# Adding two of VectorE's three exponent readings by a DMA that GpSimd starts, in a fused attention and feed-forward kernel

## The chip, the cores and the metric

The kernel runs on one core of a Trainium2 chip. The metric is device time in microseconds (us) of one execution; the time before is the median of three runs. Five engines each run their own in-order list: TensorE (PE in the profile, with PEld for its weight loads), VectorE (DVE), ScalarE (ACT), GpSimd (POOL) and SyncE (SP, which here only starts DMAs). They wait for each other by semaphores.

## The reference

```python
xn = (x - mean) / sqrt(var + 1e-5)                # x: 2048 tokens x 640, bfloat16
q = xn @ wq ; k = xn @ wk ; v = xn @ wv           # 32 query heads of 20, one key and one value head
p = softmax(q k^T / sqrt(20))                     # for each head, 2048 x 2048
attn = concat(p @ v) @ wo
ffn = silu(xn @ w1) @ w2                          # hidden size 1728
out = x + attn + ffn
```

## The kernel before

A scheduler in Python lays out every instruction ahead of time. It keeps a list of pending operations with an assumed duration, a priority and the operations that they depend on, plays the five engines forward, and writes each engine's list in the order that comes out. A table of 64 rows (`SEG`), one for each 32 score blocks, gives thresholds that steer it (when a block goes to VectorE, when the values' matmuls may interrupt, and so on). On the chip the lists are fixed, and only semaphore waits move them.

The work. A prologue loads x in 16 tiles of 128 tokens, computes their mean and variance (on VectorE, or on ScalarE for the tiles in `ACT_STATS`), takes the root by a Newton iteration of some ten small GpSimd instructions (`newton`), normalises, transposes (by TensorE or by a DMA transpose, the tiles in `DT`), and projects keys, values and the first queries.

The main part walks over 2048 score blocks, each 128 keys x 512 queries of one head. A step of TensorE (`do_S`, line 1133) computes 3 or 4 of them, side by side in four row strips of its array, into PSUM banks. The exponential is taken in one of two ways:

- ScalarE reads 1 to 3 banks at once and writes exp as bfloat16 into the tile E (line 1167, `sbt10`).
- VectorE, for about a third of the blocks, reads one bank and writes it clamped as int16 into Z (line 1182, `sbt11`). The bits of that integer, read as a bfloat16, are an approximate exponential. To smooth its error the kernel uses three readings of it: Z itself, and Z with two constants added (the tile Y, `sbt12`). Z has four sets of three blocks each; when a set is full, `flush_z` orders the two additions for the whole set, one on GpSimd (line 1221, two blocks of additions in 64-bit words) and the other on GpSimd or VectorE (line 1215).

The values' matmuls (`do_pv`, line 973; "PV" below) multiply E, Z and Y blocks by the values and sum in PSUM, up to four matmuls side by side in four column strips of the array, one for each head of a group. A block of ScalarE needs one matmul. A block of VectorE needs three, one for each reading, each with its own copy of V, scaled by the reading's weight (`PH`): these are entries of one list, `self.item(...)`, from which `do_pv` takes what is ready.

In the gaps the scheduler sets the query projections, the feed-forward layers and the output projection (line 872), tanh for the SiLU on ScalarE (line 1379) and its product on VectorE (line 1384). After the last score block a short tail ends the output.

Of a DMA the scheduler assumes, in `commit`, that what it brings is there 2.0 us plus the operation's own `late` after its issue has ended. Other engines' lists are built on that.

Of the kernel before, what the change touches and what calls it, by code (L numbers as in the profile page):

```python
# [8 lines left out]
BF16 = mybir.dt.bfloat16  # L9
# [39 lines left out]
OFF_LO = 45.0  # L49
PH = ((0, 1.0), (43, 0.8046875), (86, 0.625))  # L50
# [11 lines left out]
H0_STEP = 10  # L62
# [25 lines left out]
FOUR_FROM = 35  # L88
# [7 lines left out]
PV_HOLD = 12  # L96
# [3 lines left out]
DT = (5, 6, 7, 8, 9, 10, 11, 12, 14, 15)  # L100
NORM_P = 0.9
# [13 lines left out]
STD_COST = 7.4  # L115
K1_ENG = "pool"
PV_MIN = 3
PV_GO = 9
PRO = "t0 t2 t1 p0 t3 k0 k1 p1 q1 v0 t4 k2 v1 k3 k4 t13 v2 k5 k6 v3 k7 d0"
ACT_STATS = (1, 4, 6, 12, 14, 15)  # L120
NW_ENG = ("pool", "pool", "pool")
NORM_ENG = ("pool", "dve", "dve", "dve", "pool", "dve", "dve", "dve", "dve", "pool", "dve", "pool")
# [5 lines left out]
            "ACT4", "SPLIT", "U2", "LOOK", "JOB_BANKS", "U_IDLE")  # L128
SEG = (
# [64 lines left out]
)  # L194
BATCHES = ((0, 4), (4, 10), (10, 16))
T_ACT = (0, 2, 6)


class Op:
# [1741 lines left out]
```

## Time and profile before

| | |
|---|---|
| median of 3 runs | 662.31 us (662.22 to 662.44) |
| profiled execution, time | 662.48 us |
| profiled execution, span | 660.7 us |
| granted TensorE clock | 1.000 |
| TensorE busy | 654.3 us |
| ScalarE busy | 645.8 us |
| VectorE busy | 601.5 us |
| GpSimd busy | 420.3 us |

The span runs from the first to the last instruction; the time of the same execution is 1.8 us longer. "Busy" is the union of an engine's instructions; consecutive instructions on ScalarE and TensorE overlap at their ends, so the mean duration of one is longer than the distance from one start to the next. In rows of groups the columns are: busy us, mean ns of one, idle time of the engine just ahead, and what ended most of that idle time.

### The profile page before, as it was taken

The numbers are of one execution on the slowest core, as the hardware profiler recorded it, in microseconds if no ns is written. First come the engines' busy times: TensorE is split into PE (matmuls) and PEld (weight loads), VectorE is DVE, ScalarE is ACT, GpSimd is POOL, SyncE is SP. The second block draws the span as 40 slices with busy tenths as digits, with TensorE's granted clock in tenths as the row PEclk, the third lists the DMA queues.
The fourth block names the chain that finished last, engine by engine and source line by source line (L and its number), as shares of the span: only waits on it lengthen the run. The fifth ranks groups of instructions, "written<-read, shape, count | busy, mean of one in ns | idle before, by whom it ended". The sixth has DMA issues, their size and how long they took to land.

```text
span 660.7 us, 22924 instructions
## 1 busy us (share of the span) xinstructions
PE 654.3 (99%) x9762; PEld 220.6 (33%) x9764; DVE 601.5 (91%) x1060; ACT 645.8 (98%) x735; POOL 420.3 (64%) x568
## 2 busy tenths in 40 slices
PE   8999999999999999999999999999999999999998
PEld 4432222323333333333333333333332333333334
DVE  7799999899999997999999979999999998999995
ACT  7899999999999999999999999999999999999995
POOL 6646667676776662676666744677666664766673
PEclk9999999999999999999999999999999999999999
DMA  7566300000004200001003210000000310011001
GB/s 212 97 237 195 88 18 11 10 13 13 14 20 72 73 10 10 10 10 18 18 11 57 63 39 10 18 10 8 12 19 10 77 55 25 10 18 34 11 10 42
DMA packets 52058, 27.89 MB, mean 42 GB/s; under 512 B 37910, under 2 KB 51318, under 8 KB 51958
## 3 DMA queue, kind: packets, MB, share of 16 engines
q1 hardware_dynamic: 50502, 26.22, 15.6%
q8 instruction: 78, 1.28, 0.8%
q10 hardware_dynamic: 1456, 0.22, 0.2%
q14 instruction: 22, 0.18, 0.1%
HBM read 11.44 MB, written 2.62 MB: 21 GB/s over the span
## 4 chain that ended last, share of the span: by engine, by line
PE 92%; ACT 3%; DVE 2%; DMA 2%; SPq 1%; issue 0%; DVEq 0%
PE psall L973 34%; PE psall L1133 29%; PE psall L872 27%; ACT sbt L1167 3%; DMA sbt<-sbt 1%; DVE sbt L1685 1%; DMA sbt<-in_A_x_dram 1%; SPq L1575 0%; DVE sbt L1715 0%; PE psall L1828 0%; PE psall L1369 0%; PE psall L1851 0%; ACT sbt L1379 0%; DVE sbt L1467 0%; DVE sbt L1820 0%
## 5 line engine op out<-in xcount | busy, mean ns | idle before, releaser
L1167 ACT ACTIVATE sbt<-psall 128x1024 bf16<-128x1024 f32 (+2 forms) x644 | 609.6, 1068 | 3.5 <-PE psall L1133 2.9
L1221 POOL INT64_ADD sbt<-sbt x491 | 394.1, 815 | 209.1 <-DVE sbt L1182 183.8
L1182 DVE TENSOR_SCALAR sbt<-psall 128x512 int16<-128x512 f32 x739 | 476.4, 684 | 37.1 <-PE psall L1133 27.6
L973 PE MATMUL psall<-sbt 128*32 128x512 bf16 x3526 | 266.7, 383 | 0.0
L1133 PE MATMUL psall<-sbt 32*128 32x512 bf16 x2048 | 243.6, 384 | 0.3 <-ACT sbt L1167 0.2
L872 PE MATMUL psall<-sbt 128*32 128x320 bf16 (+2 forms) x3939 | 218.3, 331 | 0.3 <-DVE sbt L1687 0.3
L1133 PEld LDWEIGHTS psall<-sbt 32*128 32x128 bf16 x2048 | 61.8, 91 | 235.2 <-issue 80.8
L872 PEld LDWEIGHTS psall<-sbt 128*32 128x32 bf16 x3939 | 85.6, 95 | 85.1 <-issue 50.2
L973 PEld LDWEIGHTS psall<-sbt 128*32 128x32 bf16 x3526 | 63.3, 95 | 99.5 <-issue 68.9
L1384 DVE SCALAR_TENSOR_TENSOR sbt<-sbt,psall 128x512 bf16<-128x512 bf16 x54 | 36.7, 682 | 6.5 <-ACT sbt L1379 6.0
L1379 ACT ACTIVATE sbt<-psall 128x512 bf16<-128x512 f32 x54 | 33.6, 629 | 0.4 <-PE psall L872 0.3
L1285 DVE CAST sbt<-psall 128x512 bf16<-128x512 f32 x32 | 21.9, 683 | 0.6 <-PE psall L973 0.4
L1275 DVE TENSOR_TENSOR sbt<-sbt 128x320 bf16<-128x320 bf16 x31 | 15.8, 510 | 0.0
L1448 DVE SCALAR_TENSOR_TENSOR sbt<-psall,sbt 128x320 bf16<-128x320 f32 x28 | 13.5, 484 | 1.6 <-PE psall L872 1.2
L848 PE MATMUL psall<-sbt 128*128 128x512 bf16 (+2 forms) x44 | 12.9, 447 | 1.4 <-DVE sbt L1624 1.2
L1467 DVE SCALAR_TENSOR_TENSOR sbt<-psall,sbt 128x320 bf16<-128x320 f32 x28 | 13.0, 482 | 1.2 <-PE psall L872 1.2
L1336 DVE TENSOR_SCALAR sbt<-psall 128x512 bf16<-128x512 f32 (+1 forms) x19 | 12.9, 678 | 0.1
L1685 DVE BATCH_NORM_STATS2 sbt<-sbt 128x6 f32<-128x320 bf16 x20 | 8.9, 471 | 3.4 <-DMA sbt<-in_A_x_dram 3.4
L1269 DVE RECIPROCAL sbt<-sbt 128x16 f32<-128x16 bf16 x31 | 7.6, 244 | 0.4 <-DMA sbt<-sbt 0.4
L848 PEld LDWEIGHTS psall<-sbt 128*128 128x128 bf16 x46 | 4.8, 112 | 7.5 <-issue 3.3
L1227 POOL TENSOR_TENSOR sbt<-sbt 128x768 int32<-128x768 int32 x4 | 5.9, 1465 | 0.5 <-DVE sbt L1182 0.5
L1464 ACT ACTIVATE sbt<-psall 128x320 bf16<-128x320 f32 x4 | 1.6, 437 | 4.4 <-PE psall L872 4.3
(72 smaller groups left out, 90.8 us busy)
## 6 DMA issues: line engine op xcount, KB each, us to landing
sbt<-in_A_x_dram SPq DMA_DIRECT2D x32, 160.0 KB, 3.7
out_dram<-sbt SPq DMA_DIRECT2D x15, 160.0 KB, 2.0
sbt<-in_B_w_dram SPq DMA_DIRECT2D x5, 432.0 KB, 5.3
sbt<-sbt SPq DMA_DIRECT2D x105, 20.0 KB
sbt<-in_B_w_dram SPq DMA_DIRECT2D x13, 160.0 KB, 3.0
sbt<-sbt SPq DMA_DIRECT2D x1, 1024.0 KB, 6.3
sbt<-sbt SPq DMA_TRANSPOSE x57, 2.5
sbt<-in_A_wo_dram SPq DMA_DIRECT2D x5, 160.0 KB, 3.0
```

The costliest lines, as they stand in the source:

```text
L848: return pe.matmul(self.bk(b, 0, n), self.zero[:, 0:P], self.zero[:, 0:n], start=True, stop=True)
L872: ins = pe.matmul(self.bk(b, 0, n, r, r + SLOT), w[:, r:r + SLOT], x, start=start, stop=stop, tile_position=(0, r), skip_group_check=True)
L973: ins = pe.matmul(self.bk(ub[k], 0, QW, r, r + SLOT), self.v[:, it.w, it.kt, :], it.x(), start=f, stop=False, tile_position=(0, r), skip_g ...
L1133: ins = pe.matmul(self.bk(bank[x]), self.kT[r:r + SLOT, kk, kt * P:(kt + 1) * P], self.qT[r:r + SLOT, g % 8, (g // 8) % 2, :], start=True, ...
L1167: return a.activation(self.E[:, b0 * QW:(b0 + na) * QW].rearrange("p (b n) -> p b n", n=QW), src, AF.Exp, scale=ACT_SCALE)
L1182: return v.tensor_scalar(self.Z[:, zs, zp * QW:(zp + 1) * QW], self.bk(bb), 0.0, ZMAX, ALU.max, ALU.min)
L1221: sc.new("pool", tp, lambda v, k=k, c=c: v.int64_add(self.Y[:, zs, k, 0:w].bitcast(I64), self.Z[:, zs, 0:w].bitcast(I64), c), zk + [("lib" ...
L1275: op = sc.new(eng, 0.067 + 16 * DH / 960.0, lambda v: v.tensor_tensor(dst, ut[:, :, :, 0:DH], rb, ALU.mult), [key, ("rL", up)], [("o", h0 ...
L1285: sc.new("dve", t_dve_ps(QW), lambda v: v.tensor_copy(self.U[:, up, :], self.bk(ub)), [("B", ub)], [("U", up)], prio=U_PRIO, name=f"Uev{g}")
L1379: sc.new("act", t_act(QW), lambda a: a.activation(t, src, AF.Tanh, scale=0.5), [("B", b)], [("tb", tp)], prio=TH_PRIO, name=f"th{c}_{fk}") ...
L1384: sc.new("dve", t_dve_ps(QW), lambda v: v.scalar_tensor_tensor(out=self.hT[0:rows, fk, :], in0=t, scalar=1.0, in1=src, op0=ALU.add, op1=AL ...
L1685: np_("dve", 0.41, lambda v, hf=hf: v.bn_stats(self.st6[:, n, hf, :], x[:, hf * 320:hf * 320 + 320]), self.xkeys(n), [("st6", n, hf)], pri ...
```

## The change

When a set of three VectorE blocks is full and both additions have been ordered, `flush_z` may now order one more operation on GpSimd: a DMA that adds Z to the first of the two Y readings, in bfloat16, in place (line 1239 of the changed kernel). For such a set the PV list gets two entries for a block, not three: the sum with one weight, and the second reading. For a set without the DMA it gets three, as before; Z and the first reading have the same weight, so that there are two copies of V. A new threshold `CB_TH` in the table decides for each set by how far GpSimd lags behind TensorE. 135 sets get the DMA.

The constants of the readings are new (`PH`, `PW`, `OFF_LO`), all 64 rows of the table are new (one is shown), and some thresholds. In the prologue GpSimd takes the root by one power instruction (`root`), the batches of tiles, the tiles of ScalarE's statistics (five for six) and the order of jobs (`PRO`) are others, and ScalarE's table load stands ahead of its two weight loads.

```diff
-OFF_LO = 45.0
-PH = ((0, 1.0), (43, 0.8046875), (86, 0.625))
+OFF_LO = 17.625
+PH = (0, 41, 87)
+PW = (1.0, 0.77734375)
...
-H0_STEP = 10
+H0_STEP = 20
...
-FOUR_FROM = 35
+FOUR_FROM = 15
...
-PV_HOLD = 12
+PV_HOLD = 16
...
-DT = (5, 6, 7, 8, 9, 10, 11, 12, 14, 15)
-NORM_P = 0.9
+DT = (4, 5, 7, 9, 10, 11, 12, 14, 15)
+NORM_P = 2.5
...
+POW_COST = 0.6
+CB_COST = 1.0
+CB_LATE = 1.0
+CB_PRIO = 3.0
+CB_TH = -9.0
...
-PRO = "t0 t2 t1 p0 t3 k0 k1 p1 q1 v0 t4 k2 v1 k3 k4 t13 v2 k5 k6 v3 k7 d0"
-ACT_STATS = (1, 4, 6, 12, 14, 15)
...
+PRO = "t2 t0 t1 p0 t3 k0 k1 p1 q1 t6 v0 k2 k3 t8 v1 t13 k4 k5 v2 k6 k7 v3 d0"
+ACT_STATS = (2, 4, 5, 12, 14)
...
-    (8.178, 1.808, 1.279, 0.2, 2, 4, 1, 2.527, 0.05, 0.93, 0.18, 32, 0.3, 0.573, 10, 6, 2, 54, 24, 30, 6, 0, 1, 0, 99, 0, 2, 0, -9),
+    (1.642, 0.699, 0.633, 0.313, 7, 5, 3, 2.06, 0.05, 0.14, 0.03, 23, 2.84, 1.295, 10, 6, 3, 54, 21, 33, 21, 0, 0, 0, 99, 0, 3, 16, 2.539),
...
-        self.v = sb([P, 3, KT, SLOT], BF16)
+        self.v = sb([P, 2, KT, SLOT], BF16)
...
-            self.item(g, j, kt, 0, lambda zs=zs, zp=zp: self.Z[:, zs, zp * QW:(zp + 1) * QW].bitcast(BF16),
-                      [("Z", zs, zp)])
...
+        both = n == ZB and self.wide and back["pool"] + 2 * tp - sc.t["pe"] < CB_TH
+        if both:
+            y0 = self.Y[:, zs, 0, 0:w].bitcast(BF16)
+            z0 = self.Z[:, zs, 0:w].bitcast(BF16)
+            yk = [("Y", zs, 0, i) for i in range(n)]
+            op = sc.new("pool", CB_COST, lambda q: q.dma_start(out=y0, in_=z0, accum_op=ALU.add), zk + yk, yk,
+                        prio=CB_PRIO, name="cb")
+            op.dma = op.lock = True
+            op.sem = self.s_cb[zs]
+            op.mode = 2 * P * w * 2
+            op.late = CB_LATE
...
         for i, (t, g, kt, j) in enumerate(self.zblocks):
+            if not both:
+                self.item(g, j, kt, 0, lambda i=i: self.Z[:, zs, i * QW:(i + 1) * QW].bitcast(BF16), [("Z", zs, i)])
             for k in range(2):
-                self.item(g, j, kt, k + 1, lambda k=k, i=i: self.Y[:, zs, k, i * QW:(i + 1) * QW].bitcast(BF16),
+                self.item(g, j, kt, k, lambda k=k, i=i: self.Y[:, zs, k, i * QW:(i + 1) * QW].bitcast(BF16),
                           [("Y", zs, k, i)])
...
+        def root(a, b_, pr):
...
+            add = np_("pool", 0.2, lambda g: g.tensor_scalar(ve, self.mv[:, a:b_, 1], EPS, None, ALU.add), mvk(a, b_),
+                      [("va", a)], prio=pr, name="eps")
+            add.then = np_("pool", POW_COST, lambda g: g.tensor_tensor(self.rstd[:, a:b_], ve, hb, ALU.pow),
+                           [("va", a), ("half",)], [("rs", a)], prio=pr, name="root")
```

What the new order does on the engines, as the two programs have it. The names: `sbt7` keys, `sbt8` the copies of V, `sbt9` queries, `sbt10` E, `sbt11` Z, `sbt12` Y; L1221 and L1225 are the same 64-bit addition (printed as ISA), two of them for a set of three blocks.

GpSimd's list in the second half of the main part, before:

```order
L1221 ISA sbt12<-sbt11 128x256 x2
L1221 ISA sbt12<-sbt11 128x768 x12
L1221 ISA sbt12<-sbt11 128x512 x2
L1221 ISA sbt12<-sbt11 128x768 x78
L1221 ISA sbt12<-sbt11 128x256 x2
L1221 ISA sbt12<-sbt11 128x768 x60
```

and in the change:

```order
L1225 ISA sbt12<-sbt11 128x768 x2
L1239 DMA sbt12<-sbt11 128x1536
L1225 ISA sbt12<-sbt11 128x768 x2
L1239 DMA sbt12<-sbt11 128x1536
L1225 ISA sbt12<-sbt11 128x768 x2
L1239 DMA sbt12<-sbt11 128x1536
L1225 ISA sbt12<-sbt11 128x768 x4
L1239 DMA sbt12<-sbt11 128x1536
```

Where long runs of additions stood, each pair of additions is followed by the start of a DMA of 128 x 1536 elements; in this stretch nearly every set has one.

TensorE's list in the same part of the program, before (L1133 are score steps, L973 PV matmuls):

```order
L1133 MATMUL psall<-sbt9,sbt7 128x512 x3
L973 MATMUL psall<-sbt10,sbt8 32x512
L973 MATMUL psall<-sbt11,sbt8 32x512
L973 MATMUL psall<-sbt10,sbt8 32x512
L973 MATMUL psall<-sbt12,sbt8 32x512
L973 MATMUL psall<-sbt11,sbt8 32x512
L973 MATMUL psall<-sbt10,sbt8 32x512
L973 MATMUL psall<-sbt12,sbt8 32x512 x2
L1133 MATMUL psall<-sbt9,sbt7 128x512 x3
```

and in the change (L1139 and L979):

```order
L1139 MATMUL psall<-sbt9,sbt7 128x512 x4
L979 MATMUL psall<-sbt10,sbt8 32x512 x2
L979 MATMUL psall<-sbt12,sbt8 32x512 x2
L979 MATMUL psall<-sbt10,sbt8 32x512
L979 MATMUL psall<-sbt12,sbt8 32x512 x3
L1139 MATMUL psall<-sbt9,sbt7 128x512 x3
```

The matmuls that read Z (`sbt11`) have gone from this place; those that read Y (`sbt12`) now depend on the DMA.

Instructions counted over both whole programs:

| | before | after |
|---|---|---|
| exp on ScalarE, 3 / 2 / 1 banks at once | 44 / 577 / 23 | 15 / 623 / 3 |
| blocks read by VectorE | 739 | 754 |
| first addition on VectorE | 5 | 9 |
| 64-bit additions on GpSimd | 491 | 494 |
| accumulating DMAs started by GpSimd | 0 | 135 |
| PV matmuls | 3526 | 3151 |
| PV steps (up to four matmuls side by side) | 889 | 818 |
| score steps (3 or 4 blocks) | 621 | 638 |
| tiles with statistics on ScalarE / VectorE | 6 / 10 | 5 / 11 |

More of the change, by code (lines that the diff above doesn't have):

```diff
@@ L115 @@
 STD_COST = 7.4
+POW_COST = 0.6
[3 more added lines that the diff above has]
+CB_TH = -9.0
+AG_NEXT = 3
 K1_ENG = "pool"
@@ L549, in alloc @@
         self.eps = sb([P, 1], F32)
+        self.half = sb([P, 1], F32)
         self.cy = sb([P, 2], I32)
@@ L1567, in prologue @@
         self.ut_cnt = [0, 0]
+        self.s_cb = [sem(f"cb{i}") for i in range(NZ)]
+        self.cb_cnt = [0] * NZ
         self.s_oT = [sem(f"oT{i}") for i in range(4)]
@@ L1576, in load_x @@
                         self.xkeys(n)[:2] if n < NT - 1 else self.xkeys(n)[:1], P * D * 2, sem=s_x[n])
-            op.late = 0.1 if n == 0 else 0.3 if n == 1 else 1.2 if n < 13 else 2.2
+            op.late = (0.1, 0.2, 0.4, 0.6)[n] if n < 4 else 1.4 if n < 13 else 2.2
             op.inc_no = 1
@@ L1587, in load_w @@
             sc.note(op, (), [tag])
+        sc.new("pool", 0.1, lambda g: g.memset(self.eps[:, :], EPS), [], [("eps",)], name="pool")
+        sc.new("act", 1.4, lambda ac: ac.activation(self.tmp[:, 1, 0:1], self.eps[:, :], AF.Exp), [("eps",)],
+               [("warm",)], prio=0.0, name="table")
         for src, k, j in ((self.A_wk, "k", 0), (self.A_wv, "v", 1)):
             sv = src.rearrange("(c p) d -> p c d", p=P)
-            load_w("act", k, [lambda q, sv=sv, j=j: q.dma_start(self.kv_st[:, j, :, :], sv)], ("st", k), 25600)
+            load_w("act", k, [lambda q, sv=sv, j=j: q.dma_start(self.kv_st[:, j, :, :], sv)], ("st", k), 25600, (),
+                   [("warm",)], 1.5 + j)
         for n in range(4):
@@ L1624, in prologue @@
         np_("dve", 0.3, lambda v: v.memset(self.zero[:, :], 0.0), [], [("zero",)], prio=-1.0, name="zero")
[L1625 removed]
+        pool(0.1, lambda g: g.memset(self.half[:, :], -0.5), [], [("half",)])
         for k in range(2):
[L1627 removed]
+            pool(0.1, lambda g, k=k: g.memset(self.cy[:, k:k + 1], PH[k + 1] * 65537), [], [("cy",)])
         pool(0.7, lambda g: g.memset(self.wk[:, :, :], 0.0), [], [("wk",), ("ost", 2, 0), ("ost", 2, 1)])
@@ L1647, in prologue @@
         pool(0.9, lambda g: g.memset(self.v[:, :, :, :], 0.0), [], [("v0",)] + [("v", i) for i in range(8)])
-        for k in range(3):
-            pool(0.15, lambda g, k=k: g.memset(self.v[:, k, :, DH:DH + 1], 0.5 * PH[k][1]), [("v0",)],
+        for k in range(2):
+            pool(0.15, lambda g, k=k: g.memset(self.v[:, k, :, DH:DH + 1], 0.5 * PW[k]), [("v0",)],
                  [("v0",)] + [("v", i) for i in range(8)])
@@ L1684, in stats @@
             for hf in range(2):
-                np_("dve", 0.41, lambda v, hf=hf: v.bn_stats(self.st6[:, n, hf, :], x[:, hf * 320:hf * 320 + 320]),
-                    self.xkeys(n), [("st6", n, hf)], prio=prio, name=f"st{n}")
-            np_("dve", 0.10, lambda v: v.bn_aggr(self.mv[:, n, :], self.st6[:, n, :, :]),
-                [("st6", n, 0), ("st6", n, 1)], [("mv", n)], prio=prio - 0.001, name=f"ag{n}")
+                last = np_("dve", 0.41, lambda v, hf=hf: v.bn_stats(self.st6[:, n, hf, :], x[:, hf * 320:hf * 320 + 320]),
+                           self.xkeys(n), [("st6", n, hf)], prio=prio, name=f"st{n}")
+            op = np_("dve", 0.10, lambda v: v.bn_aggr(self.mv[:, n, :], self.st6[:, n, :, :]),
+                     [("st6", n, 0), ("st6", n, 1)], [("mv", n)], prio=prio - 0.001, name=f"ag{n}")
+            if n == AG_NEXT:
+                last.then = op
         def mvk(a, b_):
@@ L1718, in norm @@
             op.lock = True
-            if n == self.batch[n] and n < 4 and self.last_nw.eng == eng:
-                self.last_nw.then = op
-        def newton(a, b_, pr, eng):
-            v_ = self.tmp[:, 0, a:b_]
-            y_ = self.rstd[:, a:b_]
-            w_ = self.tmp[:, 2, a:b_]
-            ch = []
-            def nw(fn, r, w):
-                ch.append(np_(eng, 0.09, fn, r, w, prio=pr, name="nw"))
-                ch[-1].lock = True
-                self.last_nw = ch[-1]
-                if len(ch) > 1:
-                    ch[-2].then = ch[-1]
-            nw(lambda v: v.tensor_scalar(v_, self.mv[:, a:b_, 1], EPS, None, ALU.add), mvk(a, b_), [("va", a)])
-            nw(lambda v: v.tensor_scalar(y_.bitcast(I32), v_.bitcast(I32), -0.5, 1597463007.0, ALU.mult, ALU.add),
-               [("va", a)], [("rs", a)])
-            m_ = self.mv[:, a:b_, 0]
-            rv, rw, rr = [("va", a)], [("w", a)], [("rs", a)]
-            nb = [("nb", n) for n in range(a, b_)]
-            for _ in range(2):
-                nw(lambda v: v.tensor_tensor(w_, y_, y_, ALU.mult), rr, rw)
-                if eng == "dve":
-                    nw(lambda v: v.scalar_tensor_tensor(out=w_, in0=w_, scalar=-0.5, in1=v_, op0=ALU.mult,
-                                                        op1=ALU.mult), rw + rv, rw)
-                    nw(lambda v: v.scalar_tensor_tensor(out=y_, in0=w_, scalar=1.5, in1=y_, op0=ALU.add,
-                                                        op1=ALU.mult), rw + rr, rr)
-                else:
-                    nw(lambda v: v.tensor_tensor(w_, w_, v_, ALU.mult), rw + rv, rw)
-                    nw(lambda v: v.tensor_scalar(w_, w_, -0.5, 1.5, ALU.mult, ALU.add), rw, rw)
-                    nw(lambda v: v.tensor_tensor(y_, w_, y_, ALU.mult), rw + rr, rr)
-            if all(NORM_ENG[n - 4] == "dve" for n in range(max(a, 4), b_)):
-                return
-            if eng == "dve":
-                nw(lambda v: v.scalar_tensor_tensor(out=self.nb[:, a:b_], in0=m_, scalar=-1.0, in1=y_, op0=ALU.mult,
-                                                    op1=ALU.mult), mvk(a, b_) + rr, nb)
-            else:
-                nw(lambda v: v.tensor_tensor(w_, m_, y_, ALU.mult), mvk(a, b_) + rr, rw)
-                nw(lambda v: v.tensor_scalar(self.nb[:, a:b_], w_, -1.0, None, ALU.mult), rw, nb)
@@ L1760, in prologue @@
-        np_("act", 1.4, lambda ac: ac.activation(self.tmp[:, 1, 0:1], self.eps[:, :], AF.Exp), [("eps",)],
-            [("warm",)], prio=0.0, name="table")
+        def root(a, b_, pr):
+            ve = self.tmp[:, 0, a:b_]
+            h = self.half[:, :]
+            hb = bass.AP(self.half, h.offset, [list(h.ap[0]), [0, b_ - a]])
+            add = np_("pool", 0.2, lambda g: g.tensor_scalar(ve, self.mv[:, a:b_, 1], EPS, None, ALU.add), mvk(a, b_),
+                      [("va", a)], prio=pr, name="eps")
+            add.then = np_("pool", POW_COST, lambda g: g.tensor_tensor(self.rstd[:, a:b_], ve, hb, ALU.pow),
+                           [("va", a), ("half",)], [("rs", a)], prio=pr, name="root")
+            add.lock = add.then.lock = True
@@ L1766, in prologue @@
                 self.batch[n] = a
-            newton(a, b_, 0.001 * i if b_ <= 4 else 0.3, NW_ENG[i])
+            root(a, b_, 0.001 * i if b_ <= 4 else 0.3)
             if b_ <= 4:
@@ L1858, in consume @@
                 sv = self.bk(b, 0, 20 * m).rearrange("p (i d) -> p i d", d=DH)
-                for k in range(3):
+                for k in range(2):
                     sc.new("dve", 0.07 + m * DH / 960.0, lambda v, k=k: v.tensor_scalar(
-                        self.v[:, k, n0:n1, 0:DH], sv, PH[k][1], None, ALU.mult),
+                        self.v[:, k, n0:n1, 0:DH], sv, PW[k], None, ALU.mult),
                         [("B", b), ("v0",)], [(kk, i) for i in range(n0 // 2, n1 // 2) for kk in ("v", "vv")], prio=0.6,
```

35 lines of the change are left out of this document (11 added, 24 removed), and 126 rows, old and new, of the table SEG.

## The prediction, as it was made before the run

> **What bounds the kernel now.** I read the page's table of engines first, then the windows along the span, the groups by line and form, and the chain of waits.
>
> ```profile
> span 660.7 us, 22924 instructions
> PE 654.3 (99%) x9762; PEld 220.6 (33%) x9764; DVE 601.5 (91%) x1060; ACT 645.8 (98%) x735; POOL 420.3 (64%) x568
> 300.00:400.00 100.00, 100.00 (x1547) 33.28 (x1539) 90.41 (x155) 99.82 (x109) 63.69 (x80) 1.00 0.16 35
> 400.00:500.00 100.00, 100.00 (x1541) 33.02 (x1538) 93.09 (x157) 99.38 (x111) 65.74 (x82) 1.00 0.05 11
> 500.00:600.00 100.00, 100.00 (x1536) 33.56 (x1533) 92.44 (x157) 99.37 (x117) 61.82 (x77) 1.00 0.16 34
> by line: PE psall L973 34.3%; PE psall L1133 29.5%; PE psall L872 27.3%; ACT sbt L1167 2.5%; DMA sbt<-sbt 1.0%; DVE sbt L1685 0.7%; DMA sbt<-in_A_x_dram 0.6%; SPq L1575 0.5%; DVE sbt L1715 0.4%; PE psall L1828 0.4%; PE psall L1369 0.4%; PE
> ```
>
> A window's columns after its length are the busy times of PE, PEld, DVE, ACT and POOL. In the main part TensorE is busy for the whole of every 100 us and ScalarE for 99.4 to 99.8: two engines bound the kernel at once. VectorE has 7 to 10 us in 100 left, GpSimd 34 to 38. A change that relieves TensorE alone gains nothing once ScalarE is the later one; it gains as much as the less relieved of the two. The chain runs nearly all over TensorE, by its PV matmuls (L973), score steps (L1133) and other jobs (L872).
>
> **What the exponentials give.** The changed table moves blocks among the forms.
>
> ```profile
> L1167 ACT ACTIVATE sbt<-psall 128x1024 bf16<-128x1024 f32 x577 | 544.5, 1054 | 2.9 <-PE psall L1133 2.5
> L1167 ACT ACTIVATE sbt<-psall 128x1536 bf16<-128x1536 f32 x44 | 65.1, 1484 | 0.5 <-PE psall L1133 0.4
> L1167 ACT ACTIVATE sbt<-psall 128x512 bf16<-128x512 f32 x23 | 14.2, 624 | 0.1
> L1182 DVE TENSOR_SCALAR sbt<-psall 128x512 int16<-128x512 f32 x739 | 476.4, 684 | 37.1 <-PE psall L1133 27.6 <-PE psall L973 0.5 <-POOL sbt L1221 0.3
> 499.38 1.03 ACT L1167 ACTIVATE sbt<-psall 128x1024 bf16<-128x1024 f32 x1
> 500.29 0.62 ACT L1379 ACTIVATE sbt<-psall 128x512 bf16<-128x512 f32 x1
> 500.76 1.06 ACT L1167 ACTIVATE sbt<-psall 128x1024 bf16<-128x1024 f32 x1
> 18.19 5.05 ACT L1167 ACTIVATE sbt<-psall 128x1536 bf16<-128x1536 f32 x4 [0.21 <-PE psall L1133]
> ```
>
> Instructions overlap at their ends, so I price them from start to start in the timeline: two banks 0.91 us (499.38 to 500.29), one bank 0.47 (500.29 to 500.76, a tanh of the same size), three banks 1.33 (the stretch at 18.19 is three of them and one of two banks: 5.05 less 1.05, over three). The counts go from 577/44/23 to 623/15/3 of two, three and one bank: +46 x 0.91 - 29 x 1.33 - 20 x 0.47 = 41.9 - 38.6 - 9.4 = **-6.1 us on ScalarE**, because 15 blocks move to VectorE and few single banks are left.
>
> VectorE pays 15 x 0.645 (476.4 / 739) = 9.7 us for these. It keeps over 5 us in 100 of room, so I count that at nothing; the cover is gone when VectorE's lag holds back the banks that score steps want.
>
> **What the PV matmuls give.**
>
> ```profile
> 502.88 1.25 PE L973 MATMUL psall<-sbt 128*32 128x512 bf16 x20
> 504.07 0.40 PE L1133 MATMUL psall<-sbt 32*128 32x512 bf16 x4
> 504.39 0.62 PE L973 MATMUL psall<-sbt 128*32 128x512 bf16 x8
> 504.94 0.39 PE L1133 MATMUL psall<-sbt 32*128 32x512 bf16 x3
> ```
>
> Twenty PV matmuls are five steps of four; with 0.39 for the last one to end, (1.25 - 0.39) / 4 = 0.215 us a step. The count of matmuls falls by 405 (three for each of 135 sets) and rises by 30, as 15 blocks go from ScalarE (one matmul) to VectorE (three): 3526 to 3151. But steps count, not matmuls, and the new list has more partly filled ones: 889 to 818, so 71 x 0.215 = -15.3 us, not a quarter of 375 matmuls (-20). The score steps go the other way, 621 to 638. A score step costs 0.32 (504.07 to 504.39), and coming back to it costs 0.55 - 2 x 0.215 = 0.12 (504.39 to 504.94, less two PV steps); +17 x 0.44 = +7.5. **TensorE: -7.8 us.** So ScalarE's 6.1 is the smaller relief, and what the main part can give.
>
> **What the DMA costs.** No DMA of GpSimd and no accumulating one is in the trace; I bound both of its prices.
>
> ```profile
> L1221 POOL INT64_ADD sbt<-sbt x491: 395/824/830, 47.3 to 649.9; - x164
> POOL sbt L1221 <- DVE sbt L1182: 183.8, 210, 6.4
> 657.95 0.37 ACTq L1471 DMA_DIRECT2D out_dram<-sbt  x1
> L1345 SPq DMA_DIRECT2D sbt<-sbt x135: 559/707/1511, 41.8 to 581.4; - x135
> L1254 SPq DMA_TRANSPOSE sbt<-sbt x31: 1189/1210/1808, 52.3 to 635.0; - x31
> out_dram<-sbt SPq DMA_DIRECT2D x15, 160.0 KB, 2.0
> sbt<-sbt SPq DMA_DIRECT2D x1, 768.0 KB, 4.4
> PEld psall L973 <- POOL sbt L1221: 13.8, 61, 0.2
> ```
>
> *On GpSimd's queue.* Starting a DMA takes 0.37 us on ScalarE's queue, 0.71 (median) on SyncE's between tiles in SBUF, 1.21 for a transpose. I take 0.9, between the last two, and 0.37 and 1.21 as ends; on GpSimd software may do more of it, so the upper end isn't firm. Behind it wait the next set's additions, and behind those TensorE's PV matmuls. The room: 491 additions lie between 47.3 and 649.9, that is 602.6 / 245 = 2.46 us for a set of two, of which they take 2 x 0.824 = 1.65; 0.81 is left, and today GpSimd spends it waiting for VectorE (183.8 us in 210 waits). Where every set has a DMA, 0.9 is slightly too much; over all 247 sets 135 x 0.9 = 122 us fits into 247 x 0.81 = 200. The densest stretch, counted in GpSimd's list, has 65 DMAs in 75 sets: room for 75 x 0.81 / 65 = 0.93 each. So at 0.9: nothing on the path.
>
> *Until the data is there.* The order expects it 1.0 (start) + 2.0 + 1.0 (`CB_LATE`) = 4.0 us after the start. The DMA writes 393 KB and reads both Z and Y, 786 KB. Rows: 160 KB in 2.0 us, 768 KB between tiles in SBUF in 4.4. On the line through the two, 393 KB take 2.9; with both reads counted, 4.4. I take 3.6: in time. Above 4.0 TensorE's in-order list stands at the PV matmul, and with it the score step behind, on which ScalarE waits. Now PV matmuls' weight loads wait for an addition 61 times in 245 sets, 0.23 us each, and TensorE covers them. With 135 sets behind a DMA the same share is 34 waits x 0.23 = 7.7 us if nothing covered them, 0 if all were; a landing spreads more than an addition's end, and I take **+1.5**.
>
> The Trainium skill (DMA: Bandwidth & Descriptors, Anatomy of one DMA, SWDGE path) gives a DMA that GpSimd starts 2.0 us plus its bytes at 436 GB/s. By it 393 KB would take an estimated 2.9 us and the two reads 3.8, both inside the 4.0, and the sum would lose its +1.5. The trace's 4.4 us for 768 KB is longer than the 3.8 that it gives, so I stay with the rows.
>
> **What the prologue gives.**
>
> ```profile
> 16.06 0.73 ACT L1670 ACTIVATE sbt<-sbt 128x640 bf16<-128x640 bf16 x1
> 16.80 0.47 ACT L1313 ACTIVATE sbt<-psall,sbt 128x256 bf16<-128x256 f32 x1
> 23.79 1.94 ACT L1167 ACTIVATE sbt<-psall 128x1024 bf16<-128x1024 f32 x2 [0.55 <-PE psall L1133]
> 26.22 5.24 ACT L1167 ACTIVATE sbt<-psall 128x1024 bf16<-128x1024 f32 x7 [0.49 <-PE psall L1133]
> 31.98 8.49 ACT L1167 ACTIVATE sbt<-psall 128x1024 bf16<-128x1024 f32 x9 [0.52 <-PE psall L1133]
> ```
>
> One tile of statistics less on ScalarE is two readings of 0.74 us (16.06 to 16.80), 1.5 us, just ahead of the first exponential at 18.19, where ScalarE had idled only 0.21. It shortens the start by 0 (score steps not earlier) to 1.5; I take half, **-0.7**. After that ScalarE waits 0.55 + 0.49 + 0.52 = 1.56 us for score steps while tiles are still being transposed. The other order of tiles may save these or double them: -1.6 to +1.6, taken at 0. The root by one power instruction takes ten GpSimd steps off the path to the first tile; it is inside that 0.7. The tail's operations are the same.
>
> **The sum.** -6.1 - 0.7 + 1.5 = -5.3 us against the profiled execution's own 662.48 (span 660.7 and 1.8 around it): 657.2. That execution is 0.17 above the median of the runs, so 657.0.
>
> **The rivals.**
> 1. *The forecast*, ScalarE's relief: 657.0. Chance 0.50.
> 2. *Everything comes through*: no late landing, the full 1.5 of the prologue and its three waits gone: -6.1 - 1.5 - 1.6 = -9.2, 653.1. TensorE's -7.8 with the same 3.1 of the prologue doesn't stop it. For it: GpSimd's present room. Chance 0.12.
> 3. *GpSimd becomes the bound* (slower). The place is the dense stretch, the point 0.93 us for a start. At the transposes' 1.21 it gives back 65 x 0.28 = 18 us: 675. The gain is used up at 0.93 + 5.3 / 65 = 1.01. Against it: a shorter SyncE start (0.71). For it: how little lies between 0.9 and 1.01. Chance 0.20.
> 4. *Late landings* (slower). At 4.4 us, 0.4 over, if the 34 sets above wait 0.4 each it is 14 us in place of 1.5: 669.5; all 135, 54 us. It decides from 4.2, where 34 x 0.2 is the gain. For it: the two reads. Chance 0.10.
> 5. *VectorE holds up the starts* (slower).
>
> ```profile
> L1275 DVE TENSOR_TENSOR sbt<-sbt 128x320 bf16<-128x320 bf16 x31 | 15.8, 510 | 0.0
> L1215 DVE TENSOR_SCALAR sbt<-sbt 128x1536 int16<-128x1536 int16 x5 | 2.7, 550 | 0.0
> ```
>
> VectorE's instructions between tiles in SBUF, 31 normalisations of 0.51 us and now 9 first additions of 0.55, would each keep GpSimd from starting a DMA: 40 x 0.5 = 20 us at most, 11 with 135 of 247 sets, 668. Against it: GpSimd's additions last 824 of at most 830 ns with VectorE busy 92%, none stretched. The Trainium skill (SBUF — State Buffer, section SBUF: two separate sides) states that VectorE in a two-port mode locks GpSimd out of writing descriptors; no run here shows a descriptor yet. Chance 0.03.
> 6. *The gains are just used up*: within 0.2%, about what a measurement of this kernel tells from no change. Chance 0.05.
>
> That the DMAs were not ordered is excluded: 135 stand in GpSimd's list.
>
> **How the numbers follow.** Faster by over 0.2%: 0.50 + 0.12 = 0.62. Within: 0.05. Slower: 0.20 + 0.10 + 0.03 = 0.33. The range begins below rival 2 at 652, which leaves out about 0.04, and ends at 676, just above rival 3 at the transposes' price; beyond lie starts of over 1.2 us and most sets landing late, some 0.15.
>
> **What would show it.** Right: ScalarE's group of two-bank exponentials x623 at about 0.91 from start to start, ScalarE over 99% busy in the windows, GpSimd at about 80 of 100 us with waits for VectorE left, hardly any wait of TensorE for a DMA. Wrong by rival 3: GpSimd's row of additions waits for no one and its windows are full from 300 us on. By rival 4: TensorE or its weight loads at PV wait for a DMA of tiles, and exponentials wait for score steps. By rival 5: the DMA starts on GpSimd differ widely in length and the long ones lie beside VectorE's normalisations. A first exponential later than 18.2 us would show the prologue's term wrong.

## The result and the profile after

The changed kernel takes 685.5 us (median of four runs, 677.8 to 689.8) against 662.4 for the kernel before: 1.031 times as long, 95% interval 1.022 to 1.040. (The ratio leaves out one run with a lower clock.) That is slower where I forecast faster, and above the range. The profiled execution took 684.04 us.

The page of the changed kernel, its windows (columns: length, busy time of PE, PEld, DVE, ACT, POOL, granted clock, DMA share, GB/s) and its chain by line:

```profile
span 682.2 us, 22415 instructions
PE 653.3 (96%) x9391; PEld 215.6 (32%) x9391; DVE 612.4 (90%) x1077; ACT 643.7 (94%) x728; POOL 545.9 (80%) x681
300.00:400.00 100.00, 96.30 (x1450) 31.37 (x1446) 92.67 (x160) 96.31 (x105) 85.78 (x105) 1.00 0.59 113
400.00:500.00 100.00, 99.32 (x1480) 31.89 (x1472) 93.75 (x158) 98.99 (x113) 81.65 (x101) 1.00 0.62 118
500.00:600.00 100.00, 94.74 (x1393) 30.66 (x1389) 86.49 (x146) 94.82 (x107) 85.28 (x104) 1.00 0.86 161
PE psall L979 22%; PE psall L1139 19%; DMA sbt<-sbt 17%; PE psall L878 16%; POOL sbt L1225 9%; DVE sbt L1188 6%; POOL sbt L1239 3%; POOL sbt L1731 2%; DVE sbt L1403 1%; DVE sbt L1731 0%; POOL sbt L1742 0%; DVE sbt L1294 0%; SPq L1759 0%; DVE sbt L1304 0%; DVE sbt L1486 0%
```

Neither TensorE nor ScalarE is full any more: both lose 3.7 to 5.3 us in 100 in two of the three windows, together, so something makes both wait. The chain says what: a DMA between tiles in SBUF holds 17% of it, where it held 1.0%, and GpSimd's additions (L1225) 9%. The groups by line and form (busy, mean ns | idle before, and what ended it) and the answer on the DMA's own line:

```profile
L1173 ACT ACTIVATE sbt<-psall 128x1024 bf16<-128x1024 f32 x623 | 589.7, 1047 | 25.1 <-PE psall L1139 23.3
L1225 POOL INT64_ADD sbt<-sbt x494 | 439.3, 994 | 88.6 <-DVE sbt L1188 59.8 <-DVE sbt L1294 21.4 <-PE psall L979 4.0
L979 PE MATMUL psall<-sbt 128*32 128x512 bf16 x3151 | 253.9, 387 | 16.0 <-DMA sbt<-sbt 15.5 <-DVE sbt L1403 0.2
```

```profile
L1239 POOL DMA_DIRECT2D sbt<-sbt x135: 852/927/1334, 70.9 to 628.5; - x135
...
who waited for it (us, times):
  PEld psall L979: 21.5, 27
  PE psall L979: 15.5, 19
  DVE sbt L1188: 6.4, 7
...
DMA to landing us min/median/max: 3.8/4.6/6.9
```

The DMA lands 4.6 us after its start in the median, and of the 135, counted in the trace, 115 land after the 4.0 that the order expects. TensorE's PV matmuls wait for it 15.5 us and their weight loads 21.5, mostly the same time: 24.0 us with the overlap counted once. (Of the matmuls that read Y, only those of the sum depend on the DMA; the second reading doesn't.) ScalarE waits 23.3 us for score steps that stand behind them (2.5 before). In TensorE's timeline one such wait looks like this, PV (L979) against the score steps (L1139) in one list:

```profile
212.78 0.40 PE L979 MATMUL psall<-sbt 128*32 128x512 bf16 x4
214.65 0.40 PE L979 MATMUL psall<-sbt 128*32 128x512 bf16 x4 [1.47 <-DMA sbt<-sbt]
214.98 0.39 PE L1139 MATMUL psall<-sbt 32*128 32x512 bf16 x3
```

GpSimd's additions still wait 59.8 us for VectorE, so GpSimd has time left: a set of one DMA and two additions that waits for nothing takes 2.37 us from start to start (median of 66 in this trace), 0.77 more than two additions at 0.80.

A second loss is in the prologue. The first score matmul comes 1.38 us earlier than before (16.38 us against 17.76, starts of L1139 and L1133), but block 192 starts 4.7 us later. GpSimd's timeline there:

```profile
18.55 5.20 POOL L1731 TENSOR_SCALAR sbt<-sbt 128x640 bf16<-128x640 bf16 x2
23.85 0.93 POOL L1822 TENSOR_SCALAR sbt<-sbt 128x256 bf16<-128x256 bf16 x2
26.48 5.16 POOL L1731 TENSOR_SCALAR sbt<-sbt 128x640 bf16<-128x640 bf16 x2
```

Four normalisations (L1731) last 2.6 us each; in the kernel before four of the same shape took 0.88:

```profile
L1711 POOL TENSOR_SCALAR sbt<-sbt 128x640 bf16<-128x640 bf16 x4 | 3.5, 875 | 0.0
```

Copies of the keys (L1822) stand behind them. And the clock that was 1.00 throughout before is not any more:

```profile
24.00:28.00 4.00, 3.62 (x20) 0.97 (x20) 2.68 (x6) 1.93 (x2) 3.74 (x5) 0.59 0.58 86
210.00:220.00 10.00, 8.54 (x99) 2.07 (x96) 7.25 (x14) 7.22 (x9) 6.08 (x9) 0.83 0.85 179
```

The records of the granted clock give 0.5 for 3.41 us three times, from 24.7, 215.9 and 239.8 us, each after TensorE had stood for 1.47, 1.47 and 1.78 us.

My theory after this: the landing is later than the order assumes, and TensorE's list, worked off in order, waits for it; and GpSimd's normalisation has a dear form. The rivals: GpSimd's starts are the bound; the DMA's traffic slows everything, waited for or not; the new order is bad by itself.

### The profile page after: what moved, and what is told of

Read it like the earlier page. It is cut to its first block, busy times and chain, and to the rows that moved or that the text cites. A ratio compares the mean times of both kernels' runs of the same rounds, so it can differ in the third digit from the quotient of the medians.

```text
span 682.2 us, 22415 instructions
## 1 busy us (share of the span) xinstructions
PE 653.3 (96%) x9391; PEld 215.6 (32%) x9391; DVE 612.4 (90%) x1077; ACT 643.7 (94%) x728; POOL 545.9 (80%) x681
## 4 chain that ended last, share of the span: by engine, by line
PE 58%; DMA 17%; POOL 14%; DVE 8%; issue 2%; SPq 0%; DVEq 0%; POOLq 0%
PE psall L979 22%; PE psall L1139 19%; DMA sbt<-sbt 17%; PE psall L878 16%; POOL sbt L1225 9%; DVE sbt L1188 6%; POOL sbt L1239 3%; POOL sbt L1731 2%; DVE sbt L1403 1%; DVE sbt L1731 0%; POOL sbt L1742 0%; DVE sbt L1294 0%; SPq L1759 0%; DVE sbt L1304 0%; DVE sbt L1486 0%
## 5 line engine op out<-in xcount | busy, mean ns | idle before, releaser
L1173 ACT ACTIVATE sbt<-psall 128x1024 bf16<-128x1024 f32 (+1 forms) x641 | 610.6, 1055 | 26.6 <-PE psall L1139 24.7
L1188 DVE TENSOR_SCALAR sbt<-psall 128x512 int16<-128x512 f32 x754 | 488.5, 684 | 55.8 <-PE psall L1139 38.5
L1225 POOL INT64_ADD sbt<-sbt x494 | 439.3, 994 | 88.6 <-DVE sbt L1188 59.8
L979 PE MATMUL psall<-sbt 128*32 128x512 bf16 x3151 | 253.9, 387 | 16.0 <-DMA sbt<-sbt 15.5
L1139 PE MATMUL psall<-sbt 32*128 32x512 bf16 x2048 | 250.9, 386 | 4.7 <-POOL sbt L1822 1.9
L878 PE MATMUL psall<-sbt 128*32 128x320 bf16 (+2 forms) x3939 | 226.7, 331 | 1.5 <-DMA sbt<-sbt 0.6
L1239 POOL DMA_DIRECT2D sbt<-sbt x135 | 141.0, 1044 | 19.7 <-DVE sbt L1294 8.5
L1139 PEld LDWEIGHTS psall<-sbt 32*128 32x128 bf16 x2048 | 63.5, 91 | 244.4 <-issue 101.9
L878 PEld LDWEIGHTS psall<-sbt 128*32 128x32 bf16 x3939 | 84.5, 95 | 85.9 <-issue 53.9
L979 PEld LDWEIGHTS psall<-sbt 128*32 128x32 bf16 x3151 | 58.9, 95 | 116.3 <-issue 72.2
L1294 DVE TENSOR_TENSOR sbt<-sbt 128x320 bf16<-128x320 bf16 x31 | 15.3, 495 | 0.0
L854 PE MATMUL psall<-sbt 128*128 128x512 bf16 (+6 forms) x45 | 13.1, 433 | 1.2 <-DVE sbt L1649 1.2
L1731 POOL TENSOR_SCALAR sbt<-sbt 128x640 bf16<-128x640 bf16 x4 | 10.4, 2594 | 0.2
L1261 POOL INT64_ADD sbt<-sbt x1 | 0.3, 293 | 9.6 <-issue 9.6
```

The costliest lines, as they stand in the source:

```text
L878: ins = pe.matmul(self.bk(b, 0, n, r, r + SLOT), w[:, r:r + SLOT], x, start=start, stop=stop, tile_position=(0, r), skip_group_check=True)
L979: ins = pe.matmul(self.bk(ub[k], 0, QW, r, r + SLOT), self.v[:, it.w, it.kt, :], it.x(), start=f, stop=False, tile_position=(0, r), skip_g ...
L1139: ins = pe.matmul(self.bk(bank[x]), self.kT[r:r + SLOT, kk, kt * P:(kt + 1) * P], self.qT[r:r + SLOT, g % 8, (g // 8) % 2, :], start=True, ...
L1173: return a.activation(self.E[:, b0 * QW:(b0 + na) * QW].rearrange("p (b n) -> p b n", n=QW), src, AF.Exp, scale=ACT_SCALE)
L1188: return v.tensor_scalar(self.Z[:, zs, zp * QW:(zp + 1) * QW], self.bk(bb), 0.0, ZMAX, ALU.max, ALU.min)
L1225: sc.new("pool", tp, lambda v, k=k, c=c: v.int64_add(self.Y[:, zs, k, 0:w].bitcast(I64), self.Z[:, zs, 0:w].bitcast(I64), c), zk + [("lib" ...
```

## The experiments

All but the two with a table of their own keep, on every engine, the order of the kernel that they start from.

**Fewer bytes in the DMA, another form of the normalisation, and both.** The second edit is written here for GpSimd's case alone; VectorE's normalisations stay as they are.

```diff
-            y0 = self.Y[:, zs, 0, 0:w].bitcast(BF16)
-            z0 = self.Z[:, zs, 0:w].bitcast(BF16)
+            y0 = self.Y[:, zs, 0, 0:64].bitcast(BF16)
+            z0 = self.Z[:, zs, 0:64].bitcast(BF16)
```

```diff
-                xa(n), self.xslot(n), self.mv[:, n, 0:1], self.rstd[:, n:n + 1], ALU.subtract, ALU.mult),
+                xa(n), self.xslot(n), self.rstd[:, n:n + 1], self.mv[:, n, 0:1], ALU.mult, ALU.add),   # GpSimd's four
```

> The changed kernel with its instruction lists as they are, but each of the 135 DMAs adds only the first 64 of 1536 columns (the rest of the first two thirds isn't added; the output lacks it). The start on GpSimd stays, the bytes fall from 393 KB to 16 KB. Late landings (my theory for the main part): the 15.5 + 21.5 us in which TensorE and its weight loads wait for the DMA go, the clock's dips to 0.5 at 210 to 250 us go, the landing falls below 4.0 us, and the time to about 668 (684 less some 16; the six of the prologue stay). GpSimd's starts as the bound (rival): 135 starts stay, so the time stays within 2 us of the changed kernel's, 682 to 686. The new order being worse by itself: also 682 to 686.

> The changed kernel, but GpSimd's four normalisations multiply by the root and add the mean in place of subtracting the mean and multiplying (values differ from the reference's in those four tiles); the order is the same. If the form (subtract, mult) is what makes one last 2.59 us where the kernel before took 0.88 for (mult, add), they fall to about 0.9 us, score block 192 starts no later than 1 us behind the kernel before (4.7 behind now) and the time falls by 5 to 7 us, to about 678. If the two per-partition operands or the place are what costs, they stay at 2.6 us and the time stays at 684.

> Both edits of the two runs above together (first 64 columns alone added by the DMA; mean added instead of subtracted in GpSimd's four normalisations). If late landings and the prologue's normalisations are the whole of the loss, they add up: 684 - 16 - 6 = 662 or lower, and with the relief of ScalarE that I predicted, 655 to 660, below the kernel before. If the order is worse by itself, the time stays over 670.

Measured on one chip, beside 662.5 for the kernel before: 660.4 (ratio 0.997, 0.996 to 0.999), 673.8 (1.016, 1.013 to 1.019) and 656.7 us (0.991, 0.989 to 0.992). With 64 columns the landing is

```profile
DMA to landing us min/median/max: 2.0/2.4/4.3
```

and three of 135 land after 4.0; nothing on TensorE waits for it. The dips of the clock at 210 to 250 us are gone; one of 10.24 us is left in the prologue, from 33.4 us. The 135 starts were kept, and 25 us came back: GpSimd's starts are not the bound. The 25 us are 9 more than I had expected, and the normalisation's 11.7 is 5 more (block 192 starts 1.65 us late, not under 1); with the landing early the normalisation is worth 660.4 - 656.7 = 3.7. So the two together cost more than their sum, by 8 us with these runs, but by as little as 1 with the later ones of a quick form (675.7 to 680.5, below), and the changed kernel's own runs spread over 12. With both gone, the windows of the main part are full again; ahead of them the engines' busy times of that run:

```profile
PE 645.5 (99%) x9388; PEld 214.5 (33%) x9391; DVE 610.8 (93%) x1077; ACT 638.3 (98%) x728; POOL 538.9 (82%) x681
300.00:400.00 100.00, 99.99 (x1503) 32.17 (x1499) 96.44 (x168) 99.70 (x111) 88.07 (x108) 1.00 0.20 37
400.00:500.00 100.00, 99.92 (x1513) 32.63 (x1509) 93.25 (x156) 99.80 (x113) 86.65 (x107) 1.00 0.20 17
500.00:600.00 100.00, 99.70 (x1521) 33.74 (x1517) 90.97 (x154) 99.14 (x113) 90.10 (x111) 1.00 0.25 37
```

and the time is the 657 of my forecast. The new order is not bad: with a landing in time it gives 5.9 us, in a kernel that leaves out most of the sum.

**A copy in place of the addition, and a third of the bytes.** Out: `accum_op=ALU.add`; and in the other run 512 columns for 1536.

> The changed kernel, but each of the 135 DMAs copies Z to Y without adding (the first two thirds' sum is lost): the same bytes written, one read fewer. If the second read sets the landing (the line through both reads gave 4.4 us, through one 2.9), its median falls from 4.6 us to about 3.4, and the time to about 670. If the landing is set by what is written and by the start, it stays at 4.4 to 4.6 and the time at 682 to 686.

> The changed kernel with each of the 135 DMAs adding only the first 512 of 1536 columns (131 KB; the rest of the sum is left out). If the landing grows with the bytes from the 2.4 us at 16 KB to the 4.4 to 4.6 us at 393 KB, it is 2.4 + 2.1 x 448/1472 = 3.0 us here, below the 4.0 that the order assumes, and the time is that of the 64-column run, 660 to 661. If accumulating adds a fixed piece to the landing, its median is over 3.5 us and the time over 665.

664.2 us (against 662.5) and 660.6 (against 662.8). The copy landed earlier and ran faster than either of my two cases. The copy of all 393 KB, its line, landing and queue:

```profile
L1239 POOL DMA_DIRECT2D sbt<-sbt x135: 553/553/862, 70.8 to 607.5; - x135
...
DMA to landing us min/median/max: 2.5/2.9/5.0
```

```profile
q0 software_dynamic: 10800, 53.09, 21.3%
```

and the addition's queue, and the landing with 512 columns:

```profile
q0 software_dynamic: 19440, 53.09, 42.0%
```

```profile
DMA to landing us min/median/max: 2.6/3.0/5.3
```

The same 53 MB take twice the engines' time when they are added, and land 1.7 us later; up to 0.4 of it is the longer start (0.93 us for 0.55, medians), as the landing counts from the start's beginning. The copy has neither the second read nor the adding, so which of these two makes the rest is not told apart. The landing grows with the bytes added, 2.4, 3.0 and 4.4 to 4.6 us for 16, 131 and 393 KB, as expected; 3, 16 and 115 of 135 are over 4.0, and the times 660.4, 660.6 and 685.5. The copy (19 over 4.0) gives 664.2. The Trainium skill (DMA: Bandwidth & Descriptors, Anatomy of one DMA, SWDGE path) gives 2.0 us plus the bytes at 436 GB/s: by that an estimated 2.9 for 393 KB, which is the copy's 2.9; the accumulating DMA's 4.6 is not covered by it.

**The form of the normalisation.** Each of GpSimd's four tiles in another form, in their order: (subtract, mult), (mult, subtract), (add, mult), (mult, add).

> The changed kernel, its order unchanged, with another form in each of GpSimd's four normalisations (128x640): tile 8 (subtract mean, mult root) as it is, tile 9 (mult root, subtract mean), tile 12 (add mean, mult root), tile 14 (mult root, add mean); three of them leave out the reference's order of operations, so only durations are read. If the subtraction is what costs, tiles 8 and 9 last 2.6 us and tiles 12 and 14 0.9. If it is an addition or subtraction that comes first, tiles 8 and 12 are the slow ones. If only (mult, add) is quick, the first three are slow.

```profile
18.55 5.18 POOL L1739 TENSOR_SCALAR sbt<-sbt 128x640 bf16<-128x640 bf16 x2
26.46 1.04 POOL L1739 TENSOR_SCALAR sbt<-sbt 128x640 bf16<-128x640 bf16 x1
28.14 0.87 POOL L1739 TENSOR_SCALAR sbt<-sbt 128x640 bf16<-128x640 bf16 x1 [0.63 <-DVE sbt L1739]
```

The first two, with a subtraction in either place, last 2.55 and 2.64 us, each by itself in the trace; those with an addition 1.04 and 0.87. The subtraction is what costs. (One run, 683.9 us.)

**The dear form alone, in the kernel before.**

```diff
-                    xa(n), self.xslot(n), self.rstd[:, n:n + 1], self.nb[:, n:n + 1], ALU.mult, ALU.add),
+                    xa(n), self.xslot(n), self.mv[:, n, 0:1], self.rstd[:, n:n + 1], ALU.subtract, ALU.mult),
```

> The kernel before with only the form of GpSimd's four normalisations changed to the changed kernel's (subtract mean, mult root); same order, same values. If this form alone is the prologue's loss where no landing is late, each of the four goes from 0.88 to 2.6 us, and the time rises by about 3.7 us (the difference between the two runs with 64 columns, 660.4 and 656.7), to 665 to 667. If the loss needed the new prologue's order, the time stays within 1 us of the kernel before.

667.4 us against 663.0, ratio 1.006 (1.005 to 1.008): 4.4 us, near the 3.7 expected. Score blocks start 5.0 us later from number 288 on and 4.9 at the end; nothing of it is made up for later. Two windows show the stretch in which 1.65 us of waiting (TensorE for L1711, from 19.5 us) become 5:

```profile
20.00:25.00 5.00, 3.33 (x17) 1.30 (x18) 0.79 (x3) 2.37 (x3) 4.67 (x7) 0.66 0.20 46
25.00:30.00 5.00, 5.00 (x47) 2.18 (x45) 3.02 (x9) 2.77 (x3) 2.39 (x11) 0.50 0.39 87
```

The clock stays at 0.5 for 10.24 us from 21.6. How much of the 5 us is the clock's is not shown: a second wait, 0.56 us for a copy of the keys (L1838), is among them, and executions with a mean clock of 0.995 took as long (667.5) as those with 0.992 (667.3).

**The quick form with the right sign.** Again written for GpSimd's case alone.

```diff
+                    g.tensor_scalar(self.nm[:, a:b_], self.mv[:, a:b_, 0], -1.0, None, ALU.mult)
...
-                xa(n), self.xslot(n), self.mv[:, n, 0:1], self.rstd[:, n:n + 1], ALU.subtract, ALU.mult),
+                xa(n), self.xslot(n), self.nm[:, n:n + 1], self.rstd[:, n:n + 1], ALU.add, ALU.mult),   # GpSimd's four
```

> The changed kernel, its order unchanged, with GpSimd's four normalisations as (add, mult) on a negated mean that one small GpSimd instruction a batch makes beforehand: it computes what the reference asks. If the subtraction is what costs, the time is that of the run with the added mean, 672 to 675, and the four last 0.9 to 1.0 us; the small instructions (two of some 0.25 us) cost less than 1 us. If the faster form worked only because it left out the order of operations, it stays at 684.

> The changed kernel with the quick form on a negated mean, again, now beside the run with the added mean on the same chip. That gave 673.8 on one chip and this 680.5 on another. If the two small instructions cost the difference, it stays at 6 to 7 us on one chip; if it was the chip (its landings), the two agree within 2 us.

> The run with the added mean in GpSimd's four normalisations, again (its values differ from the reference's in those tiles): beside the one with the negated mean on the same chip. Within 2 us of it if the chip made the difference, 6 to 7 us quicker if the two small instructions did.

680.5 us against 663.0 (ratio 1.026), 6 us over what I expected. On another chip, side by side, the two quick forms took 675.7 and 676.2 (1.019 both, 1.015 to 1.024 and 1.016 to 1.022). So the small instructions cost nothing that shows. With the full DMA the time of one kernel spreads by some us from run to run, 673.4 to 680.1 for this one on the second chip (678.6 to 681.3 on the first), while the medians of the kernel before stay within one on all of them. Whether the chip has a part in it is not shown, nor what makes a run's landings cost more: the medians of the landing are 4.5 and 4.5.

**An order that expects the median landing.** `CB_LATE` 1.6 for 1.0 and a table searched for it (all 64 rows are other), with the quick form.

> The quick normalisation form as in the run before (values as the reference asks), and another order: the late of the DMA is 1.6 in place of 1.0, so that the lists expect a landing 4.6 us after the start, which is the measured median, and a table searched for that; 109 sets take the DMA in place of 135, and two-bank, three-bank and one-bank exponentials are 620, 19 and 3 (623, 15, 3 in the changed kernel). If the waits come from the 4.0 that the order assumed, TensorE and its weight loads wait for the DMA under half of the 36.7 us that they wait with the quick form now, no clock dip follows them, and the time is well below that form's: 660 to 668. If any accumulating DMA of this size stalls TensorE whatever the order expects, by traffic rather than by the wait, the time stays at 674 or above.

681.5 us (678.1 to 692.5) against 663.4 (1.026, 1.020 to 1.032); on the same chip the changed kernel's order took 675.7 with the quick form. The waits for the DMA fell as expected, the time did not:

```profile
  PEld psall L980: 10.0, 15
  PE psall L980: 5.8, 9
```

The longest wait of TensorE is for another DMA, one of SyncE's transposes, and the one dip of the clock in the main part (3.41 us from 521.3) comes after it:

```profile
520.49 0.59 PE L879 MATMUL psall<-sbt 128*32 128x320 bf16 x12 [2.78 <-DMA sbt<-sbt]
```

That transpose (L1418) landed 6.0 us after its issue; in the same order with 64 columns (below) none of the 16 of this line took more than 4.1. So the bytes of the accumulating DMA also reach TensorE through other transfers.

**The wait away, the DMA kept; and that other order with 64 columns.** In the first, a PV matmul that would read the sum reads the keys' tile, and waits for none of these DMAs (the additions that next write the same part of Y are given the DMA as a dependency, since they no longer have it through the PV matmuls; GpSimd shows no wait for it):

```diff
+        for op in self.order["pe"]:
+            for d in [d for d in op.deps if id(d) in self.free_of]:      # free_of: the DMA -> its set's second addition
+                op.deps.discard(d)
+                op.deps.add(self.free_of[id(d)])
...
-                self.item(g, j, kt, k, lambda k=k, i=i: self.Y[:, zs, k, i * QW:(i + 1) * QW].bitcast(BF16),
+                self.item(g, j, kt, k, lambda k=k, i=i: self.kT[:, 0, i * QW:(i + 1) * QW] if both and k == 0
+                          else self.Y[:, zs, k, i * QW:(i + 1) * QW].bitcast(BF16),
```

> The kernel with the quick form and the negated mean (680.5 and 675.7 so far), its order unchanged and all 135 full DMAs as they are, but no PV matmul waits for one: where it would read the sum it reads three blocks of the keys' tile, which lie ready (the sum doesn't enter the output). Starts, bytes and traffic stay, only the wait goes. If the wait is what costs, the time falls to that of the run with 64 columns and the quick form plus what e4's traffic cost over 64 columns, 656.7 to 661, and no clock dip is left. If the traffic or the starts slow everything whether waited for or not, it stays over 670.

> The other order (late 1.6, 109 sets) with each DMA adding only the first 64 of 1536 columns (the rest of the sum is left out). It shows what that order takes by itself. If late landings still cost there, as the 15.8 us of waits left suggest, the time falls from 681.5 to 662 to 668. If that order is slow by itself, it stays over 674.

Both 666.2 us, against 663.2 (1.005, 1.003 to 1.007 and 1.003 to 1.006). The first lies between the two theories: of the 19 to 24 us that the full DMA costs over the one of 64 columns with the quick form (675.7 and 680.5 less 656.7, runs of three chips), 9.5 to 14.3 go with TensorE's wait, and 9.5 stay. Who waits for the DMA there, and that run's chain by engine:

```profile
DVE sbt L1196 <- DMA sbt<-sbt: 11.8, 18, 2.1
```

```profile
PE 68%; DMA 11%; DVE 9%; POOL 6%; ACT 3%; issue 2%; DVEq 0%; POOLq 0%; ACTq 0%
```

VectorE (L1188, L1196 in this kernel) may not write the next exponentials into a set of Z before the DMA has read it: the same late landing comes back by another way, through VectorE and the PSUM banks that it frees late. Whether all of the 9.5 is this wait, or part of it traffic (56 DMA transposes land in 3.9 us, 2.5 with 64 columns), is not told apart.

The second shows that the other order takes 9.5 us more than the changed kernel's with the quick form and 64 columns (666.2 against 656.7), and the full DMA, though expected at 4.6, another 13 to 15 (679.6 in the profiled execution, 681.5 in the median). Half of the landings are later than 4.6 (56 of 109), up to 6.9 us, and each wait for one holds a whole list; but the waits that show (5.8 us of matmuls, 3.4 of VectorE, 2.8 for the transpose) don't add up to 13, so how much is late landings and how much the traffic is not told apart.

## Why the prediction was wrong, step by step

**ScalarE's relief, -6.1 us: the price was right.** The counts are 623, 15 and 3, and in the 656.7 us run ScalarE is busy 638.3 us, 7.5 less than before; 6.1 and the 1.5 of the tile of statistics make 7.6. The time of that run is 5.9 us below the kernel before; from block 288 to the last the start of a score block moves from 1.4 us ahead to 6.6 us ahead, 5.2 of it in the main part (in between it is up to 13.6 ahead, so single blocks measure little). That this run comes out at the 657 of the forecast is partly luck: 5.2 for 6.1, 1.4 for 0.7 at the start, and nothing for the 1.5 of waits.

**TensorE's -7.8 us: the size is near, its role not shown.** In the 656.7 us run TensorE's busy time is 8.8 us less than before (645.5 for 654.3, the prologue's changes included). In the windows TensorE is busy 99.7 to 100 of 100 us and ScalarE 99.1 to 99.8. Both are full, as before, so nothing shows which of the two reliefs set the gain.

**The start, 0.9 us, and rival 3: the price was near, the bound did not come.** The start is 0.93 us in the median, but its record overlaps the next addition's; from start to start it takes 0.77, under the 0.81 of room. In the runs with 64 columns all starts stay (0.996 there) and the time is 657 to 660. Rival 5 could not come: `op.lock` in the scheduler already holds these starts and VectorE's instructions between tiles apart by waits (GpSimd's starts wait 8.5 us for L1294), and none of the 135 starts lies beside one.

**The landing, 3.6 us and +1.5 us of stalls: this is the step that failed.** I had bounded it by 2.9 and 4.4 and took a value between, below the 4.0 that decides. It is 4.4 to 4.6 for the accumulating DMA; 2.9 is what a copy takes. The bound of 4.4, from both reads, met the size by luck: the same line gives 1.5 and 2.4 us for 16 and 131 KB with both reads, and 2.4 and 3.0 were measured. And I gave the landing no spread; it goes to 6.9. Rival 4 was what happened: late landings held TensorE's list, which the run without TensorE's wait shows by the 9.5 to 14.3 us that it gains. Its price came near only by luck. 34 sets by 0.4 us gave 14 us and 669.5, and the full DMA costs 17 to 24 us over the 64 columns with the quick form (673.8 to 680.5 less 656.7); but in the trace 19 matmuls wait 0.8 us each, the clock falls after some of these waits, and 9.5 us stay without them. I gave it a chance of 0.10 because a value in the middle of the bounds stood below the threshold; with the threshold inside the bounds it should have had about a half. I had also looked only at TensorE's wait: that Z is held until the landing (11.8 us of VectorE's waits in the run without TensorE's), and that other transfers land later beside the DMA, was not in the sum; the 9.5 us that stay without TensorE's wait lie there, in shares not known.

**The prologue, -0.7 us: the second step that failed.** The start moved by 1.4 us, near the full 1.5 of the tile of statistics less; as other things changed there too, that it was the tile is not shown. But the changed form of GpSimd's normalisation was not priced at all: I took the row of the kernel before for it though the two operations in it had changed. It costs 3.7 to 4.4 us by itself, and 5 to 12 beside the late landings (685.5 less 680.5, 675.7 or 673.8, runs of several chips that spread by some us themselves). My sign for this term, a first exponential later than 18.2 us, looked at the wrong place: it came at 16.8, and the loss lay behind it.

**What I had named as a sign of rival 4** came true: "TensorE or its weight loads at PV wait for a DMA of tiles, and exponentials wait for score steps".

## What to carry to other kernels

A result that an in-order list waits for is better expected at the late end of its spread than at its middle: with the median expected, the time stayed at 681.5. No run here planned for the late end, so this is argued and not shown. Where the point that decides lies inside the bounds of an unmeasured duration, the chances belong to both sides of it. A buffer that a slow reader holds is a second wait: ask who writes it next. An instruction whose operations changed has no row in the old profile, even if engine, name and shape are the same.

## What the runs showed of the hardware

- An accumulating DMA that GpSimd starts lands in 2.4, 3.0 and 4.4 to 4.8 us (medians) for 16, 131 and 393 KB, with single ones up to 7.3; a plain copy of 393 KB in 2.9. Starting it takes GpSimd 0.85 to 1.33 us, the copy 0.55 to 0.86.
- GpSimd's normalisation of 128x640 with a subtraction in it takes 2.5 to 2.7 us, with an addition 0.86 to 1.04.
- TensorE's granted clock fell to 0.5 for 3.41 us or a multiple (6.8, 10.24) after some stretches of 1.2 to 3 us without matmuls, and not after others (1.46 us at 564 in the changed kernel, 1.91 at 553 in a run of the quick form). Twice it fell after shorter ones only: 0.23 and 0.81 us, in the other order with 64 columns, and 0.62 us, in the run with 512 columns. In the kernel before with the dear form a wait of 1.65 us and 10.24 us at 0.5 stand beside a loss of 5.
- DMA transposes that SyncE starts land in 2.5 us (median of 56) beside accumulating DMAs of 64 columns, and in 3.6 to 4.0 (medians) beside full ones, in the order of the changed kernel.
